# Three moves in the issue order of a fused linear-attention and SwiGLU kernel on one core

## The chip, the cores and the metric

The kernel runs on one core of one Trainium2 chip. The metric is device time in microseconds of one execution. The time before is 270.21 us, the median of 3 runs (269.65 to 270.88).

The core has a tensor engine (PE, with its weight loads listed apart as PEld), a vector engine (DVE), a scalar engine (ACT), GpSimd (POOL) and SyncE (SP), which here only issues transfers (DMAs). Each engine runs its own instructions in the order in which the program lists them and waits on semaphores for the others, so the order of each list is part of the kernel.

## The reference

The input `x` is one sequence of 2048 tokens by 640 features. It is normalised per token, and the same normalised `xn` feeds two branches, whose results are added to `x`:

```
xn = _layernorm(x)
return x + _A_ref(xn, A_wqkv, A_w_phi, A_wo) + _B_ref(xn, B_w1, B_w3, B_w2)

# A: linear attention, 32 heads of 20
q, k, v = split(xn @ wqkv)
phi_q = concat(softmax(q @ w_phi), softmax(-(q @ w_phi)))      # phi_k likewise from k
num = phi_q @ (phi_k^T v);  den = phi_q . sum_s(phi_k) + 1e-6
A = (num / den) @ wo
# B: SwiGLU, 640 -> 1536 -> 640
B = (silu(xn @ w1) * (xn @ w3)) @ w2
```

## The kernel before

Tokens are handled in 16 tiles of 128, and in four groups of four tiles (512 tokens). The program is written out by hand in the order of issue (`tc.manual_schedule()`); there is no planner that moves work. Semaphores between the engines and the rotation of buffers are put in by the framework. All DMAs stand in one queue, SP's. Six PSUM banks rotate through the pool `psum` (`bank`), and one two-bank tile (`pair`) is used by turns.

**First stage (lines 756 to 894): V.** For each tile the statistics of the layer norm are taken (`stats`, `ln_stats`, on DVE and POOL), the tile is normalised in place (`lx`, DVE) and transposed by a DMA into `xnT` (`by_dma`, L751). `V(t)` is the product of tile t with the V weights (L359 on PE, 10 matmuls) with its three copies out of PSUM on ACT (L374). Between these stand SwiGLU units: `unit()` takes the next pair of (group of tokens, 128 hidden features) from the list `glu`, runs 10 matmuls of 512 columns for gate and up (L461) and the tanh on ACT (L472), and gives back a function; calling it (`g6()`) issues the product on DVE (L489, L492), which frees the unit's two banks. g4 to g7 are the units of the second group of tokens, which are tiles 4 to 7. `FB(d)` then fuses the K weights with `w_phi`.

**K stage (lines 897 to 918).** `phi_unit` makes the features of a tile of K: 10 matmuls (L359, `pk`), six exponentials on ACT (L388), a row sum and a reciprocal on DVE (L422, L424), a product on POOL (L425). `kv_unit` adds the tile to the state. SwiGLU units fill the rest.

**Q stage (lines 923 to 982).** One loop of 20 rounds, t = 0 to 19. Round t, as far as it has the parts, holds in this order:

- `phi_unit(t)`: the features of tile t of Q, with `pq` on PE, and the product on POOL that ends them. Rounds 16 to 19 have no `phi_unit`.
- SwiGLU units up to round 6. From round 7 on, `out_piece(g, c)`: 128 output features of the four tiles of group g, transposed; 12 matmuls with `w2` (L642) and 5 with `wo` (L647), then a DVE addition (L650) of the transposed `x` that `x_back` (L632) brought. Groups 0 to 2 leave by this way.
- `out_unit(j)` for the four tiles 12 to 15 of the last group: token by token, 24 and 10 matmuls of 320 columns (L600), two DVE additions (L609) of the residual `xr` that `residual` loads (L146), and a store.
- `r_unit(t - 2)`: the query's product with the state (L537, 11 small matmuls on PE), which reads the transposed features `phiqT` of tile t - 2, and the quotient on DVE (L553, L556, L558) into `o_`.
- `o_transposed(t - 2)`: a DMA transpose of `o_` (L583), which the `wo` matmuls read.
- `phi_transposed(t)`: a DMA transpose of the features of tile t into `phiqT[t % 2]` (L528). It waits for POOL's product of round t and for `r_unit(t - 2)`, which reads the same half of `phiqT`. `r_unit(t)` reads it two rounds later.
- `group_back` (L657, a DMA transpose of a finished half group), `group_stored` (L146, its store), `x_back` (L632).

At round 12 every engine, SP among them, also loads the flag `ok`, which decides whether a slower, safer version follows; it does not run with these inputs.

The lines around which the change is made are these:

```
            outs = {18: (12,), 19: (13, 14, 15)}.get(t, ())
...
            if 2 <= t < NST + 2:
                r_unit(t - 2)
                o_transposed(t - 2, (t - 2) // 4)
            if t < NST:
                phi_transposed(t)
```

Of the kernel before, what the change touches and what calls it, by code (L numbers as in the profile page):

```python
# [12 lines left out]
def kernel(  # L13
# [27 lines left out]
    NST, NSC, KD, KF = S // P, S // 512, D // P, F // P  # L41
# [103 lines left out]
    def ld(dst, src):  # L145
        nc.sync.dma_start(out=dst, in_=src)  # L146
# [9 lines left out]
    with tc.manual_schedule():  # L156
        def ldT(dst, i, c):
            a = i * D + AT[c]
            nc.sync.dma_start_transpose(out=dst[:, c], in_=A_wqkv[:, a : a + P])
# [190 lines left out]
        def tile_of(t):  # L350
            return slice(t * P, (t + 1) * P)
# [17 lines left out]
        def v_unit(dst, cols, ps=None):  # L369
            for piece in chunks(by_token(cols, wv, "pv", CH, ps)):  # L370
                v_copy(dst, *piece)
# [41 lines left out]
        def phi_unit(t, w, name, exps=exps, cols=None):  # L413

            ps = by_token(cols or tile_of(t), w, name, CH)
            dst = phi[:, t % 4]
            exps(ps, dst)
            rows = dst.rearrange("p c g f -> p (c g) f")[:, :, 0:60].rearrange(
                "p a (i d) -> p a i d", d=Dh
            )  # L420
            sk = work.tile([P, 2 * NCH, 3], f32, name="sk")
            nc.vector.reduce_sum(out=sk[:], in_=rows, axis=AX.X)  # L422
            rk = work.tile([P, 2 * NCH, 3], f32, name="rk")
            nc.vector.reciprocal(out=rk[:], in_=sk[:])  # L424
            nc.gpsimd.tensor_mul(  # L425
                out=rows, in0=rows, in1=rk[:, :, :, None].to_broadcast([P, 2 * NCH, 3, Dh])
            )
# [5 lines left out]
        def phi_blocks():  # L433
            nc.vector.tensor_mul(
                out=wphi[0:FR],
                in0=wps[0:FR, :, None, :].to_broadcast([FR, NF, LH, Dh]),
                in1=mask[0:FR, None, :, None].to_broadcast([FR, NF, LH, Dh]),
            )
# [17 lines left out]
        def glu_unit(sc, fi, banks=None):  # L456

            gp, up = banks or (bank("gp")[:], bank("up")[:])
            for ps, w in ((gp, w1), (up, w3)):
                for c in range(KD):  # L460
                    nc.tensor.matmul(  # L461
                        ps,
                        w[:, c, fi * P : (fi + 1) * P],
                        xnT[:, c, sc * 512 : (sc + 1) * 512],
                        start=(c == 0),
                        stop=(c == KD - 1),
                    )
            return glu_done(sc, fi, gp, up)
# [29 lines left out]
        def kv_unit(t, v1, acc, first, last):  # L498

            for c in range(NCH):  # L500
                b, i = divmod(c, 6)
                nc.tensor.matmul(
                    acc[:, b, VC * i : VC * i + 1 + Dh * HC[c]],
                    phi[:, t % 4, c].rearrange("p g f -> p (g f)"),
                    v1[:, c, 0 : 1 + Dh * HC[c]],
                    start=(first and i == 0),
                    stop=last,
                    skip_group_check=True,
                )

        def kv_done(acc):

            for b, c0, n, k in ((0, 0, 6, 3), (1, 6, 4, 3), (1, 10, 1, 2)):
                a, e = VC * (c0 - 6 * b), 1 + Dh * k
                rows = acc[b][:, a : a + e * n].rearrange("p (c e) -> p c e", c=n)
                nc.vector.tensor_mul(
                    out=kvr[:, c0 : c0 + n, 0:k, 0:20],
                    in0=rows[:, :, 1:e].rearrange("p c (i d) -> p c i d", d=Dh),
                    in1=own[:, 0:1, 0:k, None].to_broadcast([P, n, k, Dh]),
                )  # L520
                nc.vector.tensor_mul(
                    out=kvr[:, c0 : c0 + n, 0:k, 20],
                    in0=rows[:, :, 0:1].to_broadcast([P, n, k]),
                    in1=own[:, 0:1, 0:k].to_broadcast([P, n, k]),
                )

        def phi_transposed(t):
            nc.sync.dma_start_transpose(  # L528
                out=phiqT[:, t % 2], in_=phi[:, t % 4].rearrange("p c g f -> p (c g f)")
            )  # L530
# [50 lines left out]
        def o_transposed(t, group=0):  # L581
            tau = t % 4
            nc.sync.dma_start_transpose(  # L583
                out=oTs[group][:, :, tau * P : (tau + 1) * P], in_=o_[:, t % 2]
            )

        def residual(rows):
            xr = work.tile([P, D], bf, name="xr")
            ld(xr[:], x2[rows, :])
            return xr  # L590
# [39 lines left out]
        def x_back(t):  # L630
            g, j = divmod(t, 4)
            nc.sync.dma_start_transpose(  # L632
                out=xTs[g][:, :, j * P : (j + 1) * P], in_=x2[tile_of(t), :]
            )
# [20 lines left out]
        def group_back(g, i):  # L655
            two = slice(2 * i, 2 * i + 2)
            nc.sync.dma_start_transpose(  # L657
                out=y[:, two].rearrange("p t c s -> p (t c) s"),
                in_=yTs[g % 2][:, two].rearrange("p t c s -> p (t c s)"),
            )  # L660

        def group_stored(g, i):
            rows = out2[(4 * g + 2 * i) * P : (4 * g + 2 * i + 2) * P, :]
            ld(
                rows.rearrange("(t p) d -> p t d", p=P),
                y[:, 2 * i : 2 * i + 2].rearrange("p t c s -> p t (c s)"),
            )
# [68 lines left out]
        def unit(banks=None):  # L736
            return glu_unit(*glu.pop(0), banks)
# [5 lines left out]
        def V(t, ps=None):  # L743
            v_unit(vaug[:, t], tile_of(t), ps)
# [5 lines left out]
        def by_dma(t):  # L750
            nc.sync.dma_start_transpose(out=xnT[:, :, tile_of(t)], in_=xin[:, (t // 4) % 3, t % 4, :])  # L751
# [109 lines left out]
        lx(12, 2)  # L861
        by_dma(12)
        by_dma(13)
        V(8)
        phi_blocks()
        V(9, two("pv"))
# [2 lines left out]
        V(11, two("pv"))  # L869
        ldT(wkT, 1, 4)  # L870
        ldT(wkT, 1, 5)
        g6 = unit()
        g6()
        lx(14, 2)
        by_dma(14)
# [50 lines left out]
        xrs = {}  # L926
        for t in range(NST + 4):
            if t < NST:
                phi_unit(t, wqphi, "pq")
            if t < 2:  # L930
                kv_unit(turns[t - 2], vaug[:, turns[t - 2]], acc, False, t == 1)
                if t == 1:
                    kv_done([acc[:, 0], acc[:, 1]])
                    ld(w2, B_w2.rearrange("(c p) d -> p c d", p=P))
            if t < 7:
                (fill_halves(2, 2) if t < 6 else fill(1))
                fill(1)
            for g, c in pieces.get(t, []):
                out_piece(g, c)
            if t in (16, 17):  # L940
                xrs[t - 4] = residual(tile_of(t - 4))
            outs = {18: (12,), 19: (13, 14, 15)}.get(t, ())
            for j in outs:
                last = tile_of(j) if j == NST - 1 else None
                res = out_unit(hT[:, j], tile_of(j % 4), xrs[j], last)
                if j == 12:
                    group_stored(1, 1)
                    group_back(2, 0)
                    group_back(2, 1)
                if j == 13:  # L950
                    group_stored(2, 0)
                    group_stored(2, 1)
                if j < 14:
                    xrs[j + 2] = residual(tile_of(j + 2))
                if last is None:
                    ld(out2[tile_of(j), :], res[:])
            if 2 <= t < NST + 2:
                r_unit(t - 2)
                o_transposed(t - 2, (t - 2) // 4)
            if t < NST:  # L960
                phi_transposed(t)
            if t in backs:
                group_back(*backs[t])
            if t in (12, 13):
                group_stored(0, t - 12)
            if t == 17:
                group_stored(1, 0)
            if 2 <= t < 6:
                x_back(t - 2)
            if 7 <= t < 11:  # L970
                x_back(t - 3)
            if 13 <= t < 17:
                x_back(t - 5)
            if t < 4:
                norm_unit(wqphi, 1, t)
            if t == 4:
                ld(listed[:], norms[:])
                ld(flat, listed[:].rearrange("p g -> (p g)").partition_broadcast(1))
            if t == 10:
                flag_unit()  # L980
            if t == 12:
                ok = nc.values_load(flag[0:1, 0:1], min_val=0, max_val=1)
# [55 lines left out]
```

## Time and profile before

The profile is of one execution of 269.29 us, of which the span, from the first to the last instruction, is 267.6 us.

| | |
|---|---|
| median of 3 runs | 270.21 us (269.65 to 270.88) |
| profiled execution | 269.29 us, span 267.6 us |
| PE busy | 260.6 us, 97% of the span |
| DVE / ACT / POOL busy | 73% / 43% / 34% of the span |
| granted PE clock | 0.999 of full |
| mean DMA rate | 117 GB/s |

How to read it: a busy time counts an engine's instructions from start to end. A row of the timeline has the start in us from the span's start, the time it takes, the engine, the line of the kernel, the operation, what it writes and reads, and how many instructions were merged; what the engine waited for just before stands in brackets at its end. SPq rows are DMAs being issued by SP, not the transfers themselves. PE rows overlap at their edges, because matmuls are pipelined and their ends are modelled: the time that a block of matmuls takes from the engine is read from start to start.

### The profile page before, as it was taken

What the parts mean: (1) busy time and instruction counts of PE and PEld (TensorE: products, weight loads), DVE (VectorE), ACT (ScalarE), POOL (GpSimd) and SP (SyncE); (2) the same over time, 40 slices, a digit from 0 to 9 for tenths busy, and PEclk for the clock granted to TensorE, in tenths of its full rate; (3) what the DMA queues carried; (4) which work ended last, traced back from release to release, by engine and by line L of the source; (5) the groups of instructions that cost most, each with busy time, mean ns of one, the idle gap of its engine ahead of it and who ended that gap; (6) DMA issues with size and microseconds to landing.
All of it is one profiled execution on the core that took longest, in us unless ns stands there. A gap on an engine that the chain in (4) does not pass through costs nothing. (4 is left out here: it accounts for less than half of the span.)

```text
span 267.6 us, 5009 instructions
## 1 busy us (share of the span) xinstructions
PE 260.6 (97%) x1842; PEld 154.4 (58%) x1868; DVE 194.7 (73%) x354; ACT 114.2 (43%) x348; POOL 91.1 (34%) x88
## 2 busy tenths in 40 slices
PE   8999999999999999999999999999999998999995
PEld 7766565655556555555665555555555554445763
DVE  4789974397876877799999999998799675242121
ACT  5775345736668743466766554324222420000000
POOL 5052520064544444433363333337335533000000
PEclk9999999999999999999999999999999999999999
DMA  6999957973000001500007845656966889835731
GB/s 181 259 251 182 126 117 189 325 141 85 0 0 2 1 3 13 161 2 0 0 2 212 193 103 117 93 128 152 135 141 87 187 216 141 175 73 152 174 120 55
DMA packets 83484, 31.41 MB, mean 117 GB/s; under 512 B 71935, under 2 KB 82047, under 8 KB 83456
## 3 DMA queue, kind: packets, MB, share of 16 engines
q1 hardware_dynamic: 83456, 31.05, 53.7%
q8 instruction: 16, 0.26, 0.5%
q14 instruction: 12, 0.10, 0.1%
HBM read 11.17 MB, written 2.63 MB: 52 GB/s over the span
## 5 line engine op out<-in xcount | busy, mean ns | idle before, releaser
L425 POOL TENSOR_TENSOR phi<-phi,rk 128x1320 bf16<-128x1320 bf16 x32 | 77.2, 2414 | 107.9 <-DVE rk L424 90.7
L422 DVE TENSOR_REDUCE sk<-phi 128x66 f32<-128x1320 bf16 x32 | 48.8, 1525 | 18.0 <-ACT phi L388 16.6
L461 PEld LDWEIGHTS <-w 128*128 128x128 bf16 x400 | 37.8, 98 | 40.7
L359 PEld LDWEIGHTS <-xnT 128*128 128x128 bf16 x440 | 41.7, 98 | 19.6 <-DMA xnT<-reg_h 0.8
L461 PE MATMUL up<-xnT,w 128*128 128x512 bf16 x198 | 49.6, 379 | 0.2
L461 PE MATMUL gp<-xnT,w 128*128 128x512 bf16 x185 | 48.4, 378 | 0.7
L388 ACT ACTIVATE phi<-pq 128x360 bf16<-128x360 f32 (+2 forms) x96 | 24.8, 364 | 42.2 <-issue 31.8
L642 PE MATMUL acc<-reg_h,reg_v 128*128 128x512 bf16 x180 | 41.3, 379 | 0.0
L472 ACT ACTIVATE th<-gp 128x512 f32<-128x512 f32 x47 | 28.7, 611 | 24.6 <-PE gp L461 22.8
L492 DVE SCALAR_TENSOR_TENSOR reg_h<-gs,up 128x512 bf16<-128x512 bf16 x47 | 32.3, 688 | 4.8
L489 DVE SCALAR_TENSOR_TENSOR gs<-th,gp 128x512 bf16<-128x512 f32 x47 | 30.8, 655 | 4.6 <-ACT th L472 4.6
L388 ACT ACTIVATE phi<-pk 128x360 bf16<-128x360 f32 (+2 forms) x96 | 24.9, 368 | 19.3 <-PE pk L359 19.3
L642 PEld LDWEIGHTS <-reg_v 128*128 128x128 bf16 x180 | 17.4, 98 | 19.1
L359 PE MATMUL pk<-wkphi,xnT 128*128 128x360 bf16 (+1 forms) x160 | 24.3, 299 | 0.0
L359 PE MATMUL pq<-wqphi,xnT 128*128 128x360 bf16 (+1 forms) x160 | 24.3, 299 | 0.0
L424 DVE RECIPROCAL rk<-sk 128x66 f32<-128x66 f32 x32 | 18.1, 566 | 3.2
L359 PE MATMUL pv<-reg_w,xnT 128*128 128x360 bf16 x120 | 17.3, 299 | 0.3 <-DMA xnT<-reg_h 0.3
L245 DVE BATCH_NORM_STATS2 st<-reg_h 128x6 f32<-128x320 bf16 x32 | 13.4, 477 | 3.9 <-DMA reg_h<-in_A_x_dram 3.9
L650 DVE TENSOR_TENSOR w<-acc,v_raw 128x512 bf16<-128x512 f32 x10 | 6.6, 670 | 13.1 <-DMA v_raw<-in_A_x_dram 7.3
L374 ACT CAST reg_v<-pv 128x360 bf16<-128x360 f32 (+2 forms) x36 | 9.8, 348 | 11.3 <-PE pv L359 11.3
L558 DVE TENSOR_TENSOR o__77<-pr,den 128x360 bf16<-128x360 f32 (+1 forms) x32 | 14.2, 486 | 0.5
L609 DVE TENSOR_TENSOR res<-acc,xr 128x320 bf16<-128x320 f32 (+2 forms) x8 | 3.6, 487 | 14.6 <-PE acc L600 14.6
(92 smaller groups left out, 236.6 us busy)
## 6 DMA issues: line engine op xcount, KB each, us to landing
w<-in_B_w_dram SPq DMA_DIRECT2D x2, 1280.0 KB, 6.2
reg_h<-in_A_x_dram SPq DMA_DIRECT2D x6, 320.0 KB, 4.5
reg_v<-in_B_w_dram SPq DMA_DIRECT2D x1, 1920.0 KB, 8.5
out_dram<-w SPq DMA_DIRECT2D x6, 320.0 KB, 3.3
w<-in_B_w_dram SPq DMA_DIRECT2D x4, 320.0 KB, 4.2
reg_w<-in_A_wqkv_dram SPq DMA_DIRECT2D x5, 160.0 KB, 3.7
reg_w<-in_A_wo_dram SPq DMA_DIRECT2D x1, 800.0 KB, 7.3
reg_h<-in_A_x_dram SPq DMA_DIRECT2D x4, 160.0 KB, 3.8
```

The costliest lines, as they stand in the source:

```text
L245: nc.vector.bn_stats(out=st[:, i, :], in_=xt[:, i * HD : (i + 1) * HD])
L359: nc.tensor.matmul(ps[i][:, 0 : b - a], xnT[:, c, cols], w[:, c, a:b], start=(c == 0), stop=(c == KD - 1), skip_group_check=True,)
L388: nc.scalar.activation(out=dst[:, c0 : c0 + n, g, 0:k], in_=p.rearrange("p (c f) -> p c f", c=n), func=AF.Exp, scale=1.0 - 2.0 * g,)
L422: nc.vector.reduce_sum(out=sk[:], in_=rows, axis=AX.X)
L424: nc.vector.reciprocal(out=rk[:], in_=sk[:])
L425: nc.gpsimd.tensor_mul(out=rows, in0=rows, in1=rk[:, :, :, None].to_broadcast([P, 2 * NCH, 3, Dh]))
L461: nc.tensor.matmul(ps, w[:, c, fi * P : (fi + 1) * P], xnT[:, c, sc * 512 : (sc + 1) * 512], start=(c == 0), stop=(c == KD - 1),)
L472: nc.scalar.activation(out=th[:], in_=gp, func=AF.Tanh, scale=0.5)
L489: nc.vector.scalar_tensor_tensor(out=gs[:], in0=th[:], scalar=1.0, in1=gp, op0=ALU.add, op1=ALU.mult)
L492: nc.vector.scalar_tensor_tensor(out=hT[:, 4 * sc : 4 * sc + 4, fi, :], in0=gs[:].rearrange("p (t s) -> p t s", t=4), scalar=0.5, in1=up.r ...
L558: nc.vector.tensor_mul(out=o_[:, t % 2, Dh * h0 : Dh * h1].rearrange("p (h d) -> p h d", d=Dh), in0=p3[:, :, 0:20], in1=den[:, h0:h1, None ...
L642: nc.tensor.matmul(acc4, w2[:, k, cols], hT[:, 4 * g : 4 * g + 4, k, :], start=(k == 0), stop=False,)
```

## The change

Three places change; no instruction is added and none is removed.

1. In the first stage, `g6 = unit()` (10 matmuls of 512 columns and a tanh) goes ahead of `V(8)`, where it stood behind `V(11)`. The product `g6()` stays where it was in the list.
2. In the Q stage, `phi_transposed(t)` goes ahead of `o_transposed(t - 2)` in every round that has both (2 to 15).
3. `out_unit(12)` goes from round 18 to round 16, the first without a `phi_unit`, where it stands behind `out_piece(1, 4)` and ahead of `r_unit(14)`. The residual loads, the group transposes and the stores that stood around it are spelled out anew: the load of tile 12's residual at the end of round 15, of tile 13's at the end of round 17, of tiles 14 and 15 behind `out_unit` 13 and 14; the store of tile 12 now stands ahead of `o_transposed(14)` on SP.

```
@@ first stage
         by_dma(13)
+        g6 = unit()
         V(8)
...
         ldT(wkT, 1, 5)
-        g6 = unit()
         g6()
@@ Q stage
-            if t in (16, 17):
-                xrs[t - 4] = residual(tile_of(t - 4))
-            outs = {18: (12,), 19: (13, 14, 15)}.get(t, ())
+            outs = {16: (12,), 19: (13, 14, 15)}.get(t, ())
             for j in outs:
                 last = tile_of(j) if j == NST - 1 else None
                 res = out_unit(hT[:, j], tile_of(j % 4), xrs[j], last)
-                if j == 12:
-                    group_stored(1, 1)
-                    group_back(2, 0)
-                    group_back(2, 1)
                 if j == 13:
                     group_stored(2, 0)
                     group_stored(2, 1)
-                if j < 14:
-                    xrs[j + 2] = residual(tile_of(j + 2))
+                if 13 <= j < 15:
+                    xrs[j + 1] = residual(tile_of(j + 1))
                 if last is None:
                     ld(out2[tile_of(j), :], res[:])
             if 2 <= t < NST + 2:
                 r_unit(t - 2)
-                o_transposed(t - 2, (t - 2) // 4)
             if t < NST:
                 phi_transposed(t)
+            if 2 <= t < NST + 2:
+                o_transposed(t - 2, (t - 2) // 4)
...
+            if t == 15:
+                xrs[12] = residual(tile_of(12))
+            if t == 17:
+                xrs[13] = residual(tile_of(13))
+            if t == 18:
+                group_stored(1, 1)
+                group_back(2, 0)
+                group_back(2, 1)
```

## The prediction

> **What bounds the kernel now.** I read the page first: shares, slices, then the chain that ended last.
>
> ```profile
> span 267.6 us, 5009 instructions
> ...
> PE 260.6 (97%) x1842; PEld 154.4 (58%) x1868; DVE 194.7 (73%) x354; ACT 114.2 (43%) x348; POOL 91.1 (34%) x88
> ...
> PE   8999999999999999999999999999999998999995
> ...
> PE acc L600 7%; PE acc L642 5%; PE acc L647 2%; DMA reg_w<-phi 2%; DVE sk L422 1%; PE pr L537 0%; DVE res L609 0%; SPq L583 0%; SPq L528 0%
> ```
>
> PE is full in all slices but the first, the last and the 34th (about 221 to 227 us). The chain runs from the end back through matmuls, and only in that slice leaves PE for a transfer, `reg_w<-phi`, the transposed features. No work is added or removed here, so the change is worth what it closes of PE's gaps. Next, PE's list of waits:
>
> ```profile
> PE pr L537 <- DMA reg_w<-phi: 1.0, 1, 1.0
> ...
> PE pv L359 <- DMA xnT<-reg_h: 0.3, 1, 0.3
> ```
>
> These are the two waits that the change is near. (Two others, each under 1 us, lie in the start.)
>
> **The price of the two gaps.** The list measures from the modelled end of the matmul before, so I take them from the timeline of PE, start to start. The Q stage:
>
> ```profile
> 215.19 1.24 PE L647 MATMUL acc<-w,reg_w 128*128 128x512 bf16 x5
> 216.27 0.50 PE L537 MATMUL pr<-kvr,reg_w 128*128 128x63 bf16 x11
> ...
> 221.98 2.75 PE L642 MATMUL acc<-reg_h,reg_v 128*128 128x512 bf16 x12
> 224.56 1.24 PE L647 MATMUL acc<-w,reg_w 128*128 128x512 bf16 x5
> 226.85 0.51 PE L537 MATMUL pr<-kvr,reg_w 128*128 128x63 bf16 x11 [1.04 <-DMA reg_w<-phi]
> ```
>
> In round 14 the five `wo` matmuls hold PE from 215.19 to 216.27, 1.08 us, though their row says 1.24: the next block starts before the last one's modelled end. In round 16 the same block starts at 224.56 and would have let `r_unit(14)` start at 225.64; it starts at 226.85. The gap is 1.21 us, where the list says 1.04.
>
> The first stage, with all engines:
>
> ```profile
> 26.19 3.10 SPq L751 DMA_TRANSPOSE xnT<-reg_h  x2
> ...
> 29.46 1.24 PE L461 MATMUL up<-xnT,w 128*128 128x512 bf16 x5
> 30.98 5.61 PE L359 MATMUL pv<-reg_w,xnT 128*128 128x360 bf16 x40 [0.29 <-DMA xnT<-reg_h]
> 31.67 0.69 DVE L492 SCALAR_TENSOR_TENSOR reg_h<-gs,up 128x512 bf16<-128x512 bf16 x1
> 33.06 0.69 DVE L492 SCALAR_TENSOR_TENSOR reg_h<-gs,up 128x512 bf16<-128x512 bf16 x1
> 34.66 2.55 SPq L751 DMA_TRANSPOSE xnT<-reg_h  x2
> 36.43 1.24 PE L461 MATMUL gp<-xnT,w 128*128 128x512 bf16 x4
> ...
> 38.59 1.52 PE L359 MATMUL pv<-reg_w,xnT 128*128 128x360 bf16 x10
> ```
>
> `up` of g5 starts at 29.46 and lets go at 30.54 (again 1.08); `V(8)`, whose tile lands last, starts at 30.98: 0.44 us, where the list says 0.29. Together 1.65 us by starts, 1.33 by the list. The Trainium skill, TensorE: Matmul & The Clock Gate, "Wait — 56ns, not 53.3ns?", gives 215.7 ns from start to start at 512 columns on a full clock, which for five is an estimate of 1.08; the trace agrees (1.08, clock 0.999), and by that rule the sum is the 1.65. I take 1.65 and keep 1.33 as its near end.
>
> **g6 ahead of V(8).** g6 holds PE for 38.59 - 36.43 = 2.16 us. It reads tiles 4 to 7, which `V(4)` to `V(7)` have used already. It would run from 30.54 to 32.70, and `V(8)` would start then: 1.72 us behind the 30.98 at which its tile was there. Gain 0.44. Its waits, one by one. Banks: `V(8)` now takes those of g4, whose product ends at 31.67 + 0.69 = 32.36, 0.34 us ahead of 32.70; this is the thinnest cover here, and were g4's product late, each us of it is a us of PE. `V(10)` takes g5's, free at 33.75, and starts at 32.70 + 2 x 1.36 = 35.42. Next, `V(12)` follows `V(11)` at 38.14 instead of 38.59; its transpose is the first of two issued from 34.66, against 26.19 and 30.98 for `V(8)`'s, the slowest (4.8 us): even so slow it would be 39.4, so 0 to 1.3 us could come back; it was waited for nowhere, and I take 0. On DVE the product of g6 keeps its place and has its inputs 5.9 us earlier, so it is not later. The copies on ACT follow PE.
>
> **phi's transposes ahead of o's.** SP in rounds 14 and 15, with what its transposes wait for:
>
> ```profile
> 216.64 2.41 POOL L425 TENSOR_TENSOR phi<-phi,rk 128x1320 bf16<-128x1320 bf16 x1 [2.95 <-DVE rk L424]
> ...
> 217.74 0.89 DVE L558 TENSOR_TENSOR o__77<-pr,den 128x360 bf16<-128x360 f32 x2
> ...
> 218.74 1.56 SPq L632 DMA_TRANSPOSE v_raw<-in_A_x_dram  x1
> 220.41 1.22 SPq L583 DMA_TRANSPOSE reg_v<-o__77  x1
> 221.73 1.37 SPq L528 DMA_TRANSPOSE reg_w<-phi  x1
> ...
> 229.31 0.58 SPq L146 DMA_DIRECT2D xr<-in_A_x_dram  x1
> ```
>
> Phi of tile 14 is ready at 219.05 and its transpose is issued at 221.73, 2.7 us late; SP is issuing without pause, 1.2 to 1.9 us a transpose. It lands at 226.8, when `r_unit(14)` starts. Ahead of o it goes at 220.4: 1.3 us earlier, which alone about covers the 1.21. The price is on o's: the quotient is ready at 218.63, 0.42 us before phi, so an o transpose now waits for POOL and then stands behind 1.4 us of issue, some 1.9 us late. Nobody needs it in the next round: o's of group 1 are read in round 12, of group 2 in round 17. The tight one is group 0's last, o of tile 3, read by the first `wo` matmul of round 7:
>
> ```profile
> 161.59 2.42 POOL L425 TENSOR_TENSOR phi<-phi,rk 128x1320 bf16<-128x1320 bf16 x1 [3.86 <-DVE rk L424]
> ...
> 169.71 1.63 SPq L146 DMA_DIRECT2D listed<-norms  x1
> ...
> 173.73 1.21 SPq L583 DMA_TRANSPOSE reg_v<-o__77  x1
> ...
> 177.62 1.24 PE L647 MATMUL acc<-reg_v,reg_w 128*128 128x512 bf16 x4
> ```
>
> Before it in SP's list stands a load that waits for the `listed` store; it held o until 173.73. Phi of tile 4, ready at 164.01, now goes ahead of that, so `listed` moves up by one 1.4 us issue, and with it all behind; o of tile 3 is then issued about where it was. If it is not, it goes at 175.1 and lands 2.4 us later (the median for these transposes, in the last fence below) at 177.5, against 177.62: 0 here, up to 0.3 at the bad end.
>
> The Trainium skill, DMA: Bandwidth & Descriptors, "Queues, rings and completion order", says that each DMA engine takes descriptors in ring order; by that a transpose moved ahead delays the one behind it by its own time, not only by its issue. No run here shows o behind phi yet. As a mechanism in rows: phi's transpose takes 3.1 us, 1.7 more than its 1.4 of issue, and 5.1 for tile 14 behind two others (221.73 to 226.8). 1.7 more puts o of tile 3 at 179.2 instead of 177.5, which PE would wait 1.6 us for: a rival below.
>
> **Tile 12's output into round 16.**
>
> ```profile
> 245.88 3.42 PE L600 MATMUL acc<-reg_v,reg_h 128*128 128x320 bf16 x24
> 249.14 1.52 PE L600 MATMUL acc<-reg_w,reg_v 128*128 128x320 bf16 x10
> 250.50 3.42 PE L600 MATMUL acc<-reg_v,reg_h 128*128 128x320 bf16 x24
> ```
>
> It holds PE for 4.62 us, here and there. Moved, `r_unit(14)` comes at 225.64 + 4.62 = 230.26, 3.4 us behind a transpose landed at 226.8 even without the swap. So the 1.21 is covered twice; I book it once. o of tile 12, issued at about 221.7, is read only at 225.64 + 3.26 = 228.9.
>
> What is late next is off PE. The residual of tile 12 is issued no earlier than phi of tile 15 (ready at 224.42), o, x: about 228.4 to 229.3, and lands 2.5 later, at 231 to 232. Its additions, due at 230.26, wait 1 to 1.5 us, and behind them on DVE quotient 14, on SP the store, o 14, `group_back`, the last `x_back`:
>
> ```profile
> 236.28 1.29 DVE L650 TENSOR_TENSOR w<-acc,v_raw 128x512 bf16<-128x512 f32 x2 [7.33 <-DMA v_raw<-in_A_x_dram]
> ...
> 246.80 2.91 SPq L657 DMA_TRANSPOSE w<-w  x2
> 251.48 0.36 SPq L146 DMA_DIRECT2D xr<-in_A_x_dram  x1
> ...
> 262.70 0.56 DVE L609 TENSOR_TENSOR res<-acc,xr 128x384 bf16<-128x384 f32 x1 [2.01 <-PE acc L600]
> ```
>
> The DMA view, with the median from issue to landing as the last number:
>
> ```profile
> xr<-in_A_x_dram SPq DMA_DIRECT2D x4, 160.0 KB, 2.5
> ...
> reg_w<-phi SPq DMA_TRANSPOSE x16, 3.1
> reg_v<-o__77 SPq DMA_TRANSPOSE x8, 2.4
> v_raw<-in_A_x_dram SPq DMA_TRANSPOSE x8, 3.4
> ```
>
> Additions to 232.4, quotient 14 to 234, then three issues by SP of about 1.3 us, the x transpose the last of them at 236.6, landing 3.4 later: the addition at 236.28 moves to about 240, quotient 15 to 243, the group's transposes to 250 to 253, the stores of group 2 to 254 to 256, and the load of tile 14's residual to about 256 (251.48 before); it lands at 258.5. The pieces end at 245.88 + 4.62 - 1.21 = 249.29, `out_unit(14)` at 258.5: just in time. Tile 15's residual, issued behind it, lands at about 259; the first addition that needs it comes at 262.70 - 1.21 = 261.5, so 2.5 us are to spare there. No PE bank is held up: six rotate, and the first late one is needed at 249. Booked at 0.
>
> **Sum.** 0.44 + 1.21 = 1.65 us: the profiled execution goes from 269.29 to 267.6, its span to about 266.0. The median of the runs stands 0.92 above the profiled execution; the same saving gives 270.21 - 1.65 = 268.6.
>
> **Rivals.** *One gap stays, or half of both:* tile 12's transpose (V(12)), a bank of g4, or o of tile 3 takes back 0.4 to 1.65 us: 269.0 to 270.2. For it: covers of 0.3 to 1 us. Against: PE waits for none of them now. *The list is right, not the starts:* 268.9. *Phi ahead of o costs o its whole transfer:* o of tile 3 late by 1.6, net 0.05: 270.2. *Slower:* the chain through SP at the end decides. Its place is tile 15's residual, issued behind tile 14's; from 2.5 us of slip on, each us is a us of the end. The time passes the old one by 1.35 us (0.5%) at a slip of 2.5 + 1.65 + 1.35 = 5.5, over a chain of some 27 us from 229 on; it would be 271.6 and more. For it: that chain gets longer by about 4.5 us and its transfers can each take longer than the middle. Against: a wait of 4.8 us, the slowest landing above, in place of 3.4 for each of the two x and group transposes adds only 2.8. *The change does nothing,* because the gap at round 16 appears elsewhere: phi of tile 13 is the next nearest, but is issued earlier too.
>
> **How the numbers follow.** 0.5% is 1.35 us, about what a measurement can tell from no change. Both gaps close: 0.60 (268.0 to 268.9, and some way down, since runs without the profiler are 0.9 slower and may hold larger waits of these two kinds, to 267.6). Part or all comes back: 0.27, of which o of tile 3 holds 0.05. Slower: 0.13, the end chain 0.08 of it, the rest for a wait not seen. For 8 in 10 the range reaches from 267.6 to 270.3.
>
> **What would show it.** Right: no wait of L537 on `reg_w<-phi`, `V(8)` right behind g6's `up`, `r_unit(14)` right behind L600, each `reg_w<-phi` issued within 0.1 us of POOL's end from round 7 on, a span near 266.0. Wrong: a new wait of PE on `xnT`, on DVE L492 at `V(8)`, on `reg_v<-o__77` at 177, or DVE L609 waiting for `xr` at the end.

## The result, and the profile after

The changed kernel takes 268.08 us (median of 22 runs, 267.58 to 269.45), the kernel before 269.62 us in the same comparison (22 runs, 267.87 to 270.88). The ratio is 0.9948, with a 95% interval from 0.9933 to 0.9962: 1.40 us less, between 1.0 and 1.8. (The two medians stand 1.54 us apart; savings in this text go by the ratio.) A second comparison, further below, gave 0.9966 (0.9953 to 0.9979), 0.9 us less. The forecast was 268.6 us and 1.65 us less.

The profiled execution of the changed kernel took 268.20 us. From its page, the span, the busy shares, PE's slices, and the chain that ended last with its shares:

```profile
span 266.5 us, 5010 instructions
...
PE 261.2 (98%) x1842; PEld 155.2 (58%) x1868; DVE 194.7 (73%) x354; ACT 114.2 (43%) x348; POOL 91.3 (34%) x88
...
PE   8999999999999999999999999999999999999995
...
PE 98%; issue 1%; DVE 0%
```

The hole in the 34th slice is filled, and the chain now runs along PE from the start to the last addition; before, it left PE for `reg_w<-phi`. (The trace counts one instruction more than before, 5010 against 5009; the counts of PE, DVE, ACT and POOL are unchanged.) PE's list of waits has one line left, that of the start:

```profile
PE idle L223 <- PEq L1025: 0.8, 1, 0.8
```

PE's timeline around round 16 and, in the next fence, around `V(8)`:

```profile
224.70 1.24 PE L647 MATMUL acc<-w,reg_w 128*128 128x512 bf16 x5
225.78 3.42 PE L600 MATMUL acc<-reg_v,reg_h 128*128 128x320 bf16 x24
229.04 1.52 PE L600 MATMUL acc<-reg_w,reg_v 128*128 128x320 bf16 x10
230.40 0.50 PE L537 MATMUL pr<-kvr,reg_w 128*128 128x63 bf16 x11
```

```profile
30.05 1.24 PE L461 MATMUL up<-xnT,w 128*128 128x512 bf16 x5
31.13 1.24 PE L461 MATMUL gp<-xnT,w 128*128 128x512 bf16 x5
...
32.21 1.24 PE L461 MATMUL up<-xnT,w 128*128 128x512 bf16 x5
...
33.28 6.96 PE L359 MATMUL pv<-reg_w,xnT 128*128 128x360 bf16 x50
```

In these rows everything follows without a gap: 1.08 us from the `wo` block to tile 12's output, 4.62 from there to `r_unit(14)`, 1.07 from g6's `up` to `V(8)`. The 2.16 us of g6 lie between g5 and `V(8)`, as forecast.

The chain through SP and DVE to the end, first SP's issues, then DVE's additions:

```profile
228.98 0.58 SPq L146 DMA_DIRECT2D xr<-in_A_x_dram  x1
...
236.91 1.37 SPq L632 DMA_TRANSPOSE v_raw<-in_A_x_dram  x1
...
250.34 2.93 SPq L657 DMA_TRANSPOSE w<-w  x2
...
255.74 0.46 SPq L146 DMA_DIRECT2D xr<-in_A_x_dram  x1
...
256.74 0.49 SPq L146 DMA_DIRECT2D xr<-in_A_x_dram  x1
```

```profile
231.80 0.89 DVE L609 TENSOR_TENSOR res<-acc,xr 128x320 bf16<-128x320 f32 x2 [5.13 <-DMA xr<-in_A_x_dram]
...
233.27 0.89 DVE L558 TENSOR_TENSOR o__77<-pr,den 128x360 bf16<-128x360 f32 x2
...
240.19 1.29 DVE L650 TENSOR_TENSOR w<-acc,v_raw 128x512 bf16<-128x512 f32 x2 [6.04 <-issue]
...
261.62 0.56 DVE L609 TENSOR_TENSOR res<-acc,xr 128x384 bf16<-128x384 f32 x1 [2.01 <-PE acc L600]
263.48 0.42 DVE L609 TENSOR_TENSOR res<-acc,xr 128x256 bf16<-128x256 f32 x1 [1.30 <-PE acc L600]
```

Tile 12's additions do wait for their residual, and all behind them is later than before, but the last additions wait for PE again, not for `xr`.

The last addition of the profile before is this row:

```profile
264.56 0.42 DVE L609 TENSOR_TENSOR res<-acc,xr 128x256 bf16<-128x256 f32 x1 [1.30 <-PE acc L600]
```

From the start of g5's `up` to the start of the last addition the profile before has 264.56 - 29.46 = 235.10 us, this one 263.48 - 30.05 = 233.43: 1.67 us less, against 1.65 forecast. Yet the span fell only by 1.1, because this execution reached g5's `up` 0.59 us later. So between these two profiles the sum is right to 0.02 us, while the two comparisons say 1.40 and 0.9. The experiments ask what makes up the difference, and whether each part does what the prediction says of it.

### The profile page after: what moved, and what is told of

It reads as the page before. It is cut to its first block, busy times and chain, and to the rows that moved or that the text cites. A ratio compares the mean times of both kernels' runs of the same rounds, so it can differ in the third digit from the quotient of the medians.

```text
span 266.5 us, 5010 instructions
## 1 busy us (share of the span) xinstructions
PE 261.2 (98%) x1842; PEld 155.2 (58%) x1868; DVE 194.7 (73%) x354; ACT 114.2 (43%) x348; POOL 91.3 (34%) x88
## 4 chain that ended last, share of the span: by engine, by line
PE 98%; issue 1%; DVE 0%
PE up L461 16%; PE gp L461 16%; PE acc L642 15%; PE pq L359 8%; PE pk L359 8%; PE acc L600 7%; PE pv L359 6%; PE acc L647 6%; PE gp L709 2%; PE up L709 2%; PE pr L537 2%; PE pkv L502 2%; PE pv L316 2%; PE pf L445 1%; PE idle L219 1%; PE pst L305 1%
```

## The experiments

My theory: the change is worth the two gaps of PE, each closed by its own part, the one in round 16 twice over; the end chain is hidden. Rivals: a gap closed early is given back at the next transfer; the parts act otherwise than by the gaps and add up; the end chain has no room.

### One part alone, and all together

The kernels of this group share one set of 31 runs of the kernel before (median 269.09 us).

**The seventh unit alone.**

```
         by_dma(13)
+        g6 = unit()
         V(8)
...
-        g6 = unit()
         g6()
```

> Only the seventh SwiGLU unit goes ahead of V(8); the Q stage is as before. My theory (the two gaps of PE are separate and each is worth its start-to-start size): V(8) follows g6's `up` by 1.08 us, the gap of 0.44 us is gone, L537 still waits about 1 us for `reg_w<-phi` in round 16, and the time falls by 0.44 us, 0.16% (ratio 0.9984). The rival that a shift early in the kernel is given back at the next wait for a transfer: ratio 1.000, with the wait of L537 grown to about 1.6 us.

Measured: 268.77 us, ratio 0.9995 (0.9981 to 1.0009), 0.1 us less (between 0.5 less and 0.2 more): the times allow the 0.44 us and none. In its profile `V(8)` follows g6's `up` by 1.08 us. But L537 did not wait in round 16, although nothing was changed there. PE's timeline of this kernel:

```profile
224.62 1.24 PE L647 MATMUL acc<-w,reg_w 128*128 128x512 bf16 x5
225.70 0.50 PE L537 MATMUL pr<-kvr,reg_w 128*128 128x63 bf16 x11
```

From start to start it is 1.08 us: in this execution there was no gap. So the gain was not given back at that wait in this trace, and the rival is not borne out there; the times alone do not exclude it. The 1.21 us of the profile before is not a constant of the program either.

**The order of the transposes alone.**

```
             if 2 <= t < NST + 2:
                 r_unit(t - 2)
-                o_transposed(t - 2, (t - 2) // 4)
             if t < NST:
                 phi_transposed(t)
+            if 2 <= t < NST + 2:
+                o_transposed(t - 2, (t - 2) // 4)
```

> Only phi's transposes go ahead of o's; g6 and tile 12's output are as before. My theory (the gap in round 16 is SP's lateness in issuing): phi of tile 14 is issued 1.3 to 1.6 us earlier, lands at about 225.3 to 225.6 on the clock of the profile before, and r_unit(14), due at 225.64, waits 0 to 0.2 us; the time falls by 1.0 to 1.2 us (ratio 0.9955 to 0.9963). Rival (the transfers, not the issue, are late: the 5.1 us of this transpose is a full ring): the transpose lands as late as before, and the gap stays at about 1.2 us, ratio 1.000.

Measured: 268.52 us, ratio 0.9974 (0.9957 to 0.9990), 0.7 us less. In its profile the `wo` block starts at 225.46 and `r_unit(14)` at 226.54, no gap; phi of tile 14 is issued at 221.25, 5.3 us ahead of its use, against 225.64 - 221.73 = 3.9 in the profile before. The swap closes the gap by itself, as forecast, with nothing to spare: the transpose of phi of tile 14 took 5.2 us to land in this run. The saving of 0.7 us is less than the 1.0 to 1.2 forecast, most of which its interval (0.3 to 1.2) still holds.

**Tile 12's output alone.** The change without its first and second part (the diff of the change from `outs` on, with `o_transposed` ahead of `phi_transposed` again).

> Only tile 12's output goes to round 16; g6 and the order of the transposes are as before. My theory: r_unit(14) comes at 230.3, 3.4 us behind the landing of its features, no wait of L537, and the time falls by the whole gap, 1.21 us (ratio 0.9955), as much as or 0.2 us more than by the swap alone. Rival (the chain through SP at the end binds without the swap): DVE L609 waits for `xr` at the last tiles, ratio above 0.998.

Measured: 268.04 us, ratio 0.9965 (0.9947 to 0.9984), 0.9 us less; no wait of L537, none for `xr` at the last tiles.

**The whole change again.** No edit.

> The changed kernel itself, beside the three parts on one chip. My theory: the parts are not additive, since the swap and the moved output close the same gap; the whole is worth g6 alone plus the larger of the two others, 1.65 us (ratio 0.9939), and not the sum of the three, which would be about 2.8 us (0.9895).

Measured: 268.20 us, ratio 0.9966 (0.9953 to 0.9979), 0.9 us less. The whole gives what the moved output gives alone, where the sum of the parts would be 0.1 + 0.7 + 0.9 = 1.7. With intervals of 0.3 to 0.5 us to each side the times barely tell these apart; the profiles do. From g5's `up` to the last addition the moved output alone takes 263.29 - 29.84 = 233.45 us and the whole change 233.43, so in these two profiles the swap had nothing left to close once the output was moved. That much of the theory stands. The size does not: 1.65 us lies inside the interval of the first comparison (1.0 to 1.8) and outside that of this one (0.6 to 1.3).

### The two gaps in other executions of the kernel before

No edit: the kernel before, three times, each with its profile.

> The kernel before once more, for its two gaps in another execution. Theory A (the gaps are set by the program): V(8) 0.44 us and r_unit(14) 1.21 us late, to 0.1. Theory B (they are set by how long the transfers of that execution take, so the profile before showed one draw): V(8) between 0 and 0.5 late, r_unit(14) between 0 and 1.5, together about 1.0 to 1.2 us in the mean, as the medians say; phi of tile 14 issued late where an issue of rounds 11 to 13 took over 2 us, as in the profile before (2.52), and on time where none did, as in the run with g6 alone (1.40).

> As b1: Theory A the same two gaps to 0.1 us, Theory B another draw.

> As b1: Theory A the same two gaps to 0.1 us, Theory B another draw.

PE's timelines, the first, the second and the third:

```profile
224.81 1.24 PE L647 MATMUL acc<-w,reg_w 128*128 128x512 bf16 x5
225.89 0.50 PE L537 MATMUL pr<-kvr,reg_w 128*128 128x63 bf16 x11
```

```profile
224.49 1.24 PE L647 MATMUL acc<-w,reg_w 128*128 128x512 bf16 x5
227.02 0.51 PE L537 MATMUL pr<-kvr,reg_w 128*128 128x63 bf16 x11 [1.28 <-DMA reg_w<-phi]
```

```profile
224.59 1.24 PE L647 MATMUL acc<-w,reg_w 128*128 128x512 bf16 x5
227.07 0.51 PE L537 MATMUL pr<-kvr,reg_w 128*128 128x63 bf16 x11 [1.25 <-DMA reg_w<-phi]
```

The gap is the distance of the two rows less 1.08. The table has that of `V(8)`, read in the same way, and three times of SP's transposes: how long the issue of phi of tile 11 took, how far ahead of its first possible use (the end of the `wo` block) phi of tile 14 was issued, and how long after its issue it landed, as the DMA view has it. Where the landing takes longer than the lead, the gap is the difference, to about 0.1 us.

| profile of the kernel before | time, us | gap at V(8) | gap in round 16 | issue of phi of tile 11, us long | phi of tile 14 issued ahead of use, us | landed after issue, us |
|---|---|---|---|---|---|---|
| the one of the prediction | 269.29 | 0.44 | 1.21 | 2.52 | 3.9 | 5.1 |
| first again | 268.33 | 0 | 0 | 1.34 | 5.2 | 4.8 |
| second again | 269.46 | 0 | 1.45 | 2.59 | 4.2 | 5.6 |
| third again | 269.63 | 0 | 1.40 | 2.51 | 4.3 | 5.6 |
| mean | | 0.11 | 1.02 | | | |

Theory B holds: both gaps are drawn anew in each execution. From g5's `up` to the last addition the three new executions take 233.54, 234.89 and 235.01 us, which is the 233.43 of the changed kernel and their gaps, to 0.2 us. The mean of the two gaps together, 1.13 us, lies in both measured intervals (1.0 to 1.8 and 0.6 to 1.3). It is a mean of four only. Profiles of other runs in which one of the two places is as before widen it: round 16 of the seventh unit alone had 0; `V(8)` had 0.26 in the swap alone, 0 in the moved output alone, and 0 and 0.58 in the next two runs, with an x transpose less and one more. With these the means are 0.81 and 0.16, together 0.97: about 1 us, inside the second interval and at the lower edge of the first.

A median says little about such draws. Of the 16 runs of the kernel before that the next section compares with, eight took 267.86 to 268.76 us and eight 269.46 to 269.98, with none between. That fits two outcomes of about this size, though no trace of these runs shows their gaps, and the 31 runs of the group above show no such hole.

Round 16 has two outcomes in the four profiles, none or 1.2 to 1.45, and they go with one row of SP. SP's timeline, first of the run without the gap, then of the second:

```profile
205.19 1.34 SPq L528 DMA_TRANSPOSE reg_w<-phi  x1
...
220.73 1.37 SPq L528 DMA_TRANSPOSE reg_w<-phi  x1
```

```profile
204.87 2.59 SPq L528 DMA_TRANSPOSE reg_w<-phi  x1
...
221.41 1.37 SPq L528 DMA_TRANSPOSE reg_w<-phi  x1
```

With phi of tile 11 issued in 1.34 us, phi of tile 14 goes out 224.81 + 1.08 - 220.73 = 5.2 us ahead of its use; with 2.59, 224.49 + 1.08 - 221.41 = 4.2. Of the 1.25 us that the one issue is longer, 0.68 are still there three rounds later (221.41 against 220.73), and PE comes to the place 0.32 us earlier. The rest is the landing, 5.6 us against 4.8. Together that is 1.8, of which the first run had about 0.35 to spare, and the gap is 1.45. So the late issue is only one of two terms: none of the four lands this transpose in the 3.1 us that is the median of phi's transposes, and with such a landing even the 3.9 us of the prediction's profile would have left no gap.

The run with g6 alone had 1.40 at phi of tile 11 and no gap. The moved output alone had 2.35; there phi of tile 14 landed at 221.16 + 5.9 = 227.1, 1.5 us behind the end of the `wo` block, and `r_unit(14)`, at 230.21, did not wait. Why the issue is long in some executions, no run here shows.

### One transfer less and one more ahead of phi of tile 14

These two share 16 runs of the kernel before (269.11 us).

One less:

```
-            if 13 <= t < 17:
+            if 15 <= t < 17:
                 x_back(t - 5)
```

> The kernel before without the x transposes of tiles 8 and 9 (rounds 13 and 14), so that the outputs of these two tiles get the x of tiles 0 and 1; nothing else differs. If the gap in round 16 comes from what stands ahead of phi of tile 14 in SP's queue and in the rings: that transpose is issued 1.3 to 1.6 us earlier, L537 never waits, and the time falls by the mean gap of round 16, 0.7 to 1.2 us (ratio 0.9955 to 0.9975), as the swap alone and the moved output alone do. If it comes from elsewhere: ratio 1.000.

Measured: 268.16 us, ratio 0.9975 (0.9953 to 0.9996), 0.7 us less; `wo` block at 224.45, `r_unit(14)` at 225.53, no gap. But phi of tile 11 took 1.34 us to issue in this execution, a draw in which the kernel before shows no gap either, so the verdict rests on the times: taking a transfer out of SP's list saves 0.1 to 1.3 us, in the middle as much as the swap.

One more:

```
             if 13 <= t < 17:
                 x_back(t - 5)
+            if t in (13, 14):
+                x_back(t - 5)
```

> The kernel before with the x transposes of tiles 8 and 9 issued twice each, one more transfer ahead of phi of tile 14. If SP's queue and the rings make the gap: phi of tile 14 is issued 1.3 to 1.6 us later, the gap in round 16 is 1.3 to 3 us larger, ratio 1.005 to 1.011. If not: 1.000.

Measured: 272.04 us, ratio 1.0124 (1.0085 to 1.0163), 3.3 us more. PE and, below, SP:

```profile
225.26 1.24 PE L647 MATMUL acc<-w,reg_w 128*128 128x512 bf16 x5
228.69 0.51 PE L537 MATMUL pr<-kvr,reg_w 128*128 128x63 bf16 x11 [2.18 <-DMA reg_w<-phi]
```

```profile
219.16 4.84 SPq L632 DMA_TRANSPOSE v_raw<-in_A_x_dram  x2
224.10 1.36 SPq L583 DMA_TRANSPOSE reg_v<-o__77  x1
225.55 1.38 SPq L528 DMA_TRANSPOSE reg_w<-phi  x1
```

The gap is 2.35 us in this profile, and phi of tile 14 goes out 0.8 us ahead of its use. The pair of x transposes took 4.84 us where 2.6 were meant, since the second writes where the first does and waited for its landing (4.0 us in the two waits of SP on `v_raw`). The loss is above the expected range. The profiled execution, 271.38 us, is only 2.3 us above 269.11 and has, with the 0.58 at `V(8)`, 2.93 us of gaps against 1.13 in the mean; three of the six runs took 272.7 to 273.0 us at a granted clock of 0.994, and no trace shows what they lost.

Both runs say that what stands ahead of phi of tile 14 makes the gap. It does so in two ways, which they do not separate: with an x transpose less, phi of tile 14 went out 5.6 us ahead of its use and landed 3.2 us after its issue; with one more it landed 3.1 us after its issue, and the gap is all lateness of SP. In the kernel before both terms count.

### How much room the end chain has

**The doubled x transposes in the changed kernel.** The two added lines of the edit above, put into the changed kernel.

> The changed kernel with the x transposes of tiles 8 and 9 issued twice each, beside the same in the kernel before. By my theory r_unit(14) has over 3.4 us of cover, so L537 does not wait, while tile 12's residual and with it the chain through SP at the end come 2.6 to 3.2 us later; of this the last two tiles can hide 2.5, so the time is the same to +0.5 us against the changed kernel (ratio to before 0.996 to 0.998). The rival that the end chain has no room: ratio 1.005 or more, with DVE L609 waiting for `xr` at the last tile.

Measured: 273.42 us, ratio 1.0164 (1.0132 to 1.0197), 4.4 us more than before. That is the rival's verdict, but not its test: with two such waits SP fell back much further than meant. SP, PE and DVE:

```profile
219.07 4.68 SPq L632 DMA_TRANSPOSE v_raw<-in_A_x_dram  x2
...
226.88 4.13 SPq L632 DMA_TRANSPOSE v_raw<-in_A_x_dram  x2
...
235.18 0.57 SPq L146 DMA_DIRECT2D xr<-in_A_x_dram  x1
```

```profile
225.12 1.24 PE L647 MATMUL acc<-w,reg_w 128*128 128x512 bf16 x5
...
240.23 0.49 PE L537 MATMUL pr<-kvr,reg_w 128*128 128x63 bf16 x11 [1.57 <-DVE o__77 L558]
```

```profile
267.56 0.89 DVE L609 TENSOR_TENSOR res<-acc,xr 128x384 bf16<-128x384 f32 x2 [2.41 <-DMA xr<-in_A_x_dram]
```

Tile 12's residual is issued 235.18 - 225.12 = 10.06 us behind the `wo` block, against 228.98 - 224.70 = 4.28 in the changed kernel: a slip of 5.8. Two things then bind: `r_unit(15)` waits for quotient 14, which holds the only `pr` buffer, and tile 15's additions wait for `xr`. The prediction named the second, not the first. From the `wo` block to the end of the additions it is 268.45 - 225.12 = 43.33 us, against 39.20, so 4.1 of 5.8 us were lost and 1.7 hidden. Of the 4.1, `r_unit(15)` holds 1.74 (240.23 - 225.12 = 15.11 us behind the `wo` block, against 238.07 - 224.70 = 13.37), and the end the other 2.4. To separate a room of 1.7 from the 2.5 of the prediction, two smaller slips were made that wait for no landing.

**A slip of one issue, and of two** (with 23 shared runs of the kernel before, 269.15 us):

```
             if t == 15:
+                x_back(8)
+                x_back(9)
                 xrs[12] = residual(tile_of(12))
```

The first of the two kernels has only the first added line.

> The changed kernel with one more x transpose (tile 8 again) in round 15, ahead of tile 12's residual: the chain through SP at the end starts one issue, 1.3 to 1.6 us, later, and waits for no landing. If the end has the 2.5 us to spare that the prediction worked out: no wait of DVE L609 for `xr` at tile 15, and the time of the changed kernel, ratio to before 0.995 to 0.997. If it has 1.65, as the doubled transposes suggest (5.8 us of slip, 4.1 lost): the same. If it has none: ratio 1.000 to 1.002.

> The same with two more x transposes (tiles 8 and 9 again) in round 15: a slip of 2.6 to 3.2 us. With 2.5 us to spare: 0.1 to 0.7 us lost against the changed kernel, ratio to before 0.996 to 0.999. With 1.65: 1.0 to 1.6 us lost, ratio 0.999 to 1.003, DVE L609 waits for `xr` at tile 15. With none: 2.6 to 3.2 us lost, ratio 1.005 to 1.008.

Measured: with one 268.17 us, ratio 0.9968 (0.9947 to 0.9989); with two 268.44 us, ratio 0.9964 (0.9944 to 0.9984). Neither is told from the changed kernel's 0.9966. With one, the residual slips by 1.3 us and no addition of tile 15 waits for `xr`. The two-issue kernel's SP and DVE:

```profile
231.51 0.58 SPq L146 DMA_DIRECT2D xr<-in_A_x_dram  x1
```

```profile
260.90 0.89 DVE L609 TENSOR_TENSOR res<-acc,xr 128x320 bf16<-128x320 f32 x2 [6.15 <-issue]
262.30 0.56 DVE L609 TENSOR_TENSOR res<-acc,xr 128x384 bf16<-128x384 f32 x1 [0.51 <-DMA xr<-in_A_x_dram]
263.24 0.42 DVE L609 TENSOR_TENSOR res<-acc,xr 128x256 bf16<-128x256 f32 x1 [0.38 <-PE acc L600]
```

Its `wo` block starts at 224.46, so the slip is 231.51 - 224.46 - 4.28 = 2.8 us. Here the first addition of tile 15 does wait for `xr`: it starts 262.30 - 224.46 = 37.84 us behind the `wo` block, against 261.62 - 224.70 = 36.92, so 0.9 us late, and it had 1.85 us to spare and not 2.5. The last addition still waits for PE and ends 39.20 us behind the `wo` block, as without a slip, so the whole 2.8 us are hidden. Its idle time for PE went from 1.30 us to 0.38; by these rows the end has some 3.1 us of room, an estimate. The doubled transposes hid less, 1.7 us, since `r_unit(15)` was held up there and tile 15's residual took 267.56 - 262.62 = 4.9 us from issue to use, against 262.30 - 259.25 = 3.05 here.

## Why the prediction was right, and where its size was off

**The two gaps as the whole of the change: right.** They closed, nothing opened elsewhere on PE, and in the profiles of the parts alone neither gap is left where its part was made. Starts and not the list of waits give the price: 1.67 us between the two profiles, against 1.65 by starts and 1.33 by the list. The rival "the list is right" falls for that pair.

**The sum, as the saving of many runs: the term that was off.** The step "the same saving gives 270.21 - 1.65" took the gaps of one execution for those of all. The 1.21 is 1.02 in the mean of four profiles, with one at 0; the 0.44 is 0.11, with three at 0. That makes 1.13 us, or 0.97 with the other profiles. The prediction expected larger waits in runs without the profiler, because their median stood 0.92 above; most of that 0.92 came from which three runs had been shown (with 19 more the median is 269.62, 0.33 above), and the gaps were smaller, not larger. That the time came out within 0.5 us is partly luck: the start was 0.6 us too high, and the saving taken off it was too large (1.65, against 1.40 and 0.9 in the two comparisons), so the two errors work against each other.

**g6 ahead of V(8): right in its steps, its gain not told from none.** In the changed kernel g4's product is this row:

```profile
32.26 0.69 DVE L492 SCALAR_TENSOR_TENSOR reg_h<-gs,up 128x512 bf16<-128x512 bf16 x1
```

It ends at 32.26 + 0.69 = 32.95 and `V(8)` starts at 33.28, so its bank was free 0.33 us ahead (0.34 forecast). `V(12)` followed `V(11)` without a wait.

**The transposes: right on what they cover, wrong on one of its signs.** SP's rows in the changed kernel:

```profile
173.75 1.23 SPq L583 DMA_TRANSPOSE reg_v<-o__77  x1
...
220.15 1.38 SPq L528 DMA_TRANSPOSE reg_w<-phi  x1
```

Phi of tile 14 went out at 220.15, 5.6 us ahead of its first possible use instead of 3.9. It was not issued within 0.1 us of POOL's end, as the prediction's last part had it: POOL was done at 219.19 and SP was still 1 us behind. o of tile 3, the tight one, was issued at 173.75 (173.73 before), and its `wo` block at 177.76 did not wait. The rival of ring order, for which the Trainium skill was named (DMA: Bandwidth & Descriptors, "Queues, rings and completion order"), did not bind there: o of tile 3, now behind phi, landed 2.4 us after its issue, as before, and the median of its group is 2.4 as before:

```profile
reg_w<-phi SPq DMA_TRANSPOSE x16, 3.2
reg_v<-o__77 SPq DMA_TRANSPOSE x8, 2.4
```

It is not nothing everywhere. Behind phi of tile 14, which took 5.2 us to land, o of tile 12 took 5.0, against 2.7 in the profile before, where it stood ahead of phi. It was read only at 229.04, so nobody waited. What the swap moved is the issue of phi of tile 14; it took as long to land as before (5.2 us, 5.1 before).

**Tile 12's output: right.** Covered twice, booked once: the swap alone gives 0.7 us, the moved output alone 0.9, both 0.9. With the output moved, the swap shows no gain of its own.

**The end chain: right in its steps, too strict in its price.** Forecast and measured: additions of tile 12 up to 232.4 and 232.7, the late x addition 240 and 240.2, the group's transposes 250 to 253 and 250.3 to 253.3, tile 14's residual 256 and 255.7, tile 15's first addition 2.5 us of room and 1.85. From there on, the prediction has it, each us of slip is a us of the end; that leaves out the 1.30 us that the last addition idles for PE, and a slip of 2.8 us cost nothing. What the sum left out is that quotient 14 also holds `r_unit(15)`: it ends at 234.2 in the changed kernel and is needed by 238.1, 3.9 us of cover that the doubled transposes used up.

## What to carry to other kernels

A gap in one profile is a draw: before a gap of a microsecond that ends with a transfer is booked, look at it in several more executions, or book a mean with 0 as an end. Price a gap of PE from start to start, by the same block elsewhere without the gap. Where one queue issues all transfers and is backed up, look both for the first issue that ran late and for how long the awaited transfer took to land, since either can make the gap; work that needs no transfer, put ahead of the waiting instruction, covers both, as in the moved output alone, where the features landed 1.5 us behind the end of the `wo` block.

## What the runs showed that I had not expected

The same issue of the same transpose took SP 1.34 us in one execution and 2.5 to 2.6 in three others, with no wait listed for it, and 1.2 to 1.45 us of PE three rounds later went with it, in part through a landing up to 0.8 us longer. What makes it long stays open. With both gaps covered the spread shrank too: the kernel before ran from 267.87 to 270.88 us over 22 runs, the changed one from 267.58 to 269.45; that the gaps alone make the difference in spread was not tested.
